# Products with V of four batches spread over four iterations in an attention and mixture-of-experts kernel

## The chip, the cores and the metric

The kernel runs on one core of a Trainium2 chip. The metric is the device time of one launch in microseconds (us). The core has a matrix engine (TensorE, PE in the rows; PEld are its weight loads), a vector engine (VectorE, DVE), a scalar engine (ScalarE, ACT), GpSimd (POOL) and a queue engine for transfers (SyncE, SP). Each engine runs its own instructions in program order, and they wait for each other by semaphores.

## What is computed

Attention with masks over 8 batches of 8 heads (576 positions, head size 64), then a top-1 mixture of 8 experts over the 4608 rows. Four heads see a local window of 32 positions, four see every 32nd position:

```python
scores = scale * np.matmul(q, k.transpose(0, 1, 3, 2))
mask_local = (rel >= 0) & (rel < stride)
mask_strided = (rel >= 0) & (pos[None, :] % stride == pos[:, None] % stride)
...
attn = np.exp(scores - max) / (sum + 1e-09)
attn_out = np.matmul(attn, v)
...
expert_idx = np.argmax(x @ w_gate, axis=1)        # x: attn_out, 4608 x 512
out[mask] = gate_w[mask, None] * (np.maximum(xe @ w1[e], 0.0) @ w2[e])
```

## The kernel before

**Attention** is cut into 40 tasks, five per batch (`tasks`, k = 0 to 4). Task k fills one score bank of 128 x 512: k = 0 and 1 are the two pairs of local heads, k = 2 is mixed, k = 3 and 4 are strided and their scores are issued together (`PAIR`). The loop runs one iteration per task as a software pipeline. In iteration i PE issues the transposes of the probabilities of task i - 3 (`stage_t`, `L501`), the scores of task i (`stage_s`, `L439` for the mask and `L450`, `L458`, `L464`), and the products with V of task i - 4: both pairs of local heads at k = 1 (`av_local`, `L526`), the first strided products at k = 3 and the second at k = 4 (`av_strided`, `L515`). So the products of batch b are issued while the scores of batch b + 1 are. PE's order is the order written in the code; the other engines are ordered by the scheduler.

**Softmax** of one bank: DVE takes the maximum (`nm`, `L377`) and subtracts it (`L380`, after which the score bank is free), ACT the exponential (`L381`), DVE the sum (`sm`, `L383`) and its reciprocal (`ri`, `L385`, `L386`), POOL the product (`L387`). Only then may PE transpose the probabilities. ACT copies each transposed bank (`pTl` for local heads, two copies of 64 x 512; `pT` for the others) and the products into `xT` (`L166`). There are two PSUM banks for each of the tags s (scores), t (transposes and first expert layer), v and y.

**Row work.** When all products of a batch are in `xT`, `row_steps` puts steps into `queue`: logits (`L576`), a copy `ls` by DVE (`L162`), a sum of transposed logits on PE (`L583`), rows transposed back and written to the buffer `xd` (`L568`, `L571`), and after every second batch the routing (`route`: counts with `oh`, then `am`, `bm` and `bb` on DVE, `L647` to `L659`, and the routing sum on PE, `L666`). `step()` runs one step, four times per iteration. A step that is only `single()` is a pause. For batches 0, 1, 2 the list goes to `late` and joins `queue` one iteration later, between the second and the third step of that iteration.

**Experts.** After batch 3 the first expert windows start inside the attention loop (`fillers`): gathers from `xd`, transposes (`L296`), weight chunks loaded by SP (`raw`), split by ACT and DVE into `whi` and `wlo` (`L231`, `L232`, two halves per chunk), and matmuls (`L309` to `L322`). Behind the attention loop the other windows follow.

Of the kernel before, what the change touches and what calls it, by code (L numbers as in the profile page):

```python
# [18 lines left out]
B, S, D = 8, 576, 64  # L19
# [9 lines left out]
GB = 2  # L29
# [23 lines left out]
TB = 5  # L53
EG = NG // 2
EARLY = (3, 1, 2)
X_ENG = "aa"
LS_ENG = "v"
BANKS = {"s": 2, "t": 2, "v": 2, "y": 2}
# [89 lines left out]
def moe_attn(ctx, tc, qk, vv, wg, wcat, blob0, blob, out):  # L148
# [8 lines left out]
    def bank(tag):  # L157
        return ps.tile([128, 512], F32, name=tag, bufs=BANKS[tag])

    def evac(which, out, in_):  # L160
        if which == "v":
            nc.vector.tensor_copy(out=out, in_=in_)  # L162
        elif which == "g":
            nc.gpsimd.tensor_copy(out=out, in_=in_)
        else:
            copied[0] = nc.scalar.copy(out=out, in_=in_)  # L166
# [178 lines left out]
    with ExitStack() as actx:  # L345
# [83 lines left out]
        def v_of(b, k, key, n=0):  # L429
            o = VV[k][0][key] + 128 * n  # L430
            return loaded[b, "v", k][:, o:o + 128]

        def side(k, h):

            return 1 - h if k == PAIR[1] else h
# [74 lines left out]
        def probs_of(b, pair, y, c, w):  # L510
            k, n = WHERE[pair]
            return pTs[b, k][64 * y:64 * y + 64, 128 * n + c:128 * n + c + w]

        def av_mm(av, c0, w, h, y, lhsT, rhs):
            nc.tensor.matmul(av[64 * h:64 * h + 64, c0:c0 + w], lhsT, rhs, start=True, stop=True, tile_position=(64 * y, 64 * h))  # L515

        def av_local(b, xT, off):
            for hp in range(2):
                av = bank("v")
                for m in range(2):  # L520
                    for i in range(4):
                        vt = v_of(b, hp, "l", 4 * m + i)
                        for h in range(2):
                            c = 128 * (2 * m + h) + QB * i
                            o = av[64 * h:64 * h + 64, 256 * m:256 * m + 256].rearrange("p (y r) -> p y r", y=2)
                            nc.tensor.matmul(o[:, :, QB * i:QB * i + QB], vt[:, 64 * h:64 * h + 64],  # L526
                                             pTl[hp][:, :, c:c + QB], start=True, stop=True, tile_position=(0, 64 * h))
                evac("a", xT[:, hp, off:off + 512], av)

        def av_strided(b, hp, xT, off):  # L530
            av = [bank("v"), bank("v")]
            for t in range(5):
                vst = v_of(b, WHERE["s", hp, t][0], ("s", hp, t))
                for y in range(2):
                    for h in range(2):
                        av_mm(av[y], RG * t, RG, h, y, vst[64 * y:64 * y + RG, 64 * h:64 * h + 64],
                              probs_of(b, ("s", hp, t), y, 64 * side(WHERE["s", hp, t][0], h), RG)[0:RG])
            c1 = 5 * RG
            if hp == 0:
                for i in range(2):  # L540
                    vt = v_of(b, 2, ("lx", i))
                    for y in range(2):
                        for h in range(2):
                            av_mm(av[y], c1 + QB * i, QB, h, y, vt[64 * y:64 * y + 64, 64 * h:64 * h + 64],
                                  probs_of(b, ("lx", 0, 4), y, 64 * h + 32 * i, 32))
            else:
                vst = v_of(b, 3, "sx")
                for y in range(2):
                    for h in range(2):
                        av_mm(av[y], c1, LASTG, h, y, vst[64 * y:64 * y + LASTG, 64 * h:64 * h + 64],  # L550
                              probs_of(b, ("sx", 0, 5), y, 64 * h, LASTG)[0:LASTG])
            xv = xT[:, 2 + hp, off:off + S].rearrange("p (a r) -> p r a", r=STR)
            for y in range(2):
                dst = xv[:, 0:30, :].rearrange("p (t y l) a -> p t y l a", y=2, l=3)[:, :, y, :, :]
                evac("a", dst, av[y][:, 0:c1].rearrange("p (t l a) -> p t l a", l=3, a=SR))
                if hp == 0:
                    x0 = off + 512 + QB * y
                    evac("a", xT[:, 0:2, x0:x0 + QB], av[y][:, c1:c1 + 2 * QB].rearrange("p (a q) -> p a q", q=QB))
                else:
                    xl = xT[:, 2 + y, off:off + S].rearrange("p (a r) -> p r a", r=STR)  # L560
                    evac("a", xl[:, 30:32, :], av[y][:, c1:c1 + LASTG].rearrange("p (r a) -> p r a", a=SR))

        def xrows(g, c, xT):
# [3 lines left out]
            for pr in range(4):  # L567
                nc.tensor.transpose(xb[:, pr * 128:(pr + 1) * 128], xT[:, pr, c * 128:(c + 1) * 128], ident)  # L568
            evac(X_ENG[c % 2], xr[:, 0:DM], xb)
            T = g * GT + c  # L570
# [272 lines left out]
        xTs = {}  # L843
        Ls = {}
        queue = []
        late = []

        def run(gen):
            for _ in gen:
# [2 lines left out]
        def one(fn, *a):  # L852
            fn(*a)
            yield
# [10 lines left out]
        def row_steps(g, bb, xT, L):  # L865
            lg = [logits(g, c3, xT, L) for c3 in range(bb, 1 if bb == 0 else GT // 3)]
            rows = [one(xrows, g, c, xT) for c in range(3 * bb, 3 if bb == 0 else GT)]
            last = g == NG - 1 and bb == GB - 1
            pause = [] if last or g * GB + bb < EG * GB - 1 else [single()]
            steps = list(pause)  # L870
            for r in range(3):
                steps += [part(x) for x in lg]
                if r == 0:
                    steps += [single()] if bb == 0 else pause
            if last:
                steps += rows + [route(g)]
            elif bb == GB - 1:
                steps.append(mix(route(g), rows))
                if g == EG - 1:
                    steps.append(one(lambda: fill.append(fillers())))  # L880
            else:
                steps += [x for r in rows for x in (r, single())]
            return steps
# [11 lines left out]
        def single():  # L895
            yield
# [32 lines left out]
        with tc.manual_schedule(engines={mybir.EngineType.PE}):  # L929
            for i in range(nt + LAG_AV):  # L930
                it = i - LAG_T
                if 0 <= it < nt:
                    stage_t(*tasks[it], pvs.pop(it))
                step()
                ia = i - LAG_AV
                if 0 <= ia < nt:
                    b, k = tasks[ia]
                    g, bb = divmod(b, GB)
                    if g not in xTs:
                        xTs[g] = xtp.tile([128, 4, GB * S], F32, name="xT")  # L940
                        Ls[g] = rt.tile([128, GT, E], F32, name="L", bufs=2)
                        dls[g] = rt.tile([128, GT, E], F32, name="dl", bufs=2)
                        gates[g] = rt.tile([128, GT], F32, name="gt", bufs=2)
                    step()
                exps.clear()
                if i < nt:
                    filling()
                    b, k = tasks[i]
                    if k == PAIR[0]:
                        pvs[i], pvs[i + 1] = stage_s(b, *PAIR)  # L950
                    elif k not in PAIR:
                        pvs[i], = stage_s(b, k)
                    load_qk(i + NBK)
                if 0 <= ia < nt:
                    b, k = tasks[ia]
                    if k == 0:
                        queue.extend(late)
                        late.clear()
                    elif k == 1:
                        av_local(b, xTs[g], bb * S)  # L960
                    elif k == 3:
                        av_strided(b, 0, xTs[g], bb * S)
                        for e in exps:
                            issue_after(e, copied[0])
                    elif k == 4:
                        av_strided(b, 1, xTs[g], bb * S)
                        for e in exps:
                            issue_after(e, copied[0])
                        (late if b < EG * GB - 1 else queue).extend(row_steps(g, bb, xTs[g], Ls[g]))
                        if b == B - 1:  # L970
                            filling()
                if 0 <= ia:
                    load_v(ia + NV - 1)
                step()
                filling()
                step()
# [5 lines left out]
        chain = queue.pop()  # L982
        for n in EARLY:
            with tc.high_priority():
# [326 lines left out]
```

## Time and profile before

| | |
|---|---|
| median of 3 runs | 626.51 us (624.65 to 626.82) |
| the profiled execution | 627.64 us, its span 625.9 us |
| PE busy in the span | 591.8 us (95%) |
| DVE, ACT, POOL busy | 374.8 (60%), 296.1 (47%), 160.4 us (26%) |
| mean granted clock of PE | 0.989 |

A row of a view gives a start or a stretch in us from the start of the span, a duration, an engine, a source line and the tiles written and read. Idle time stands with the engine and tile that ended it (`<-`). Rows that a prediction needs stand in a section of their own below.

### The profile page before, as it was taken

To read this page: it belongs to the slowest core of one execution; us is meant where nothing else is said; L and a number is where in the kernel's file an instruction comes from. 1 tells how busy PE (TensorE), PEld (TensorE's weight loads), DVE (VectorE), ACT (ScalarE), POOL (GpSimd) and SP (SyncE) were. 2 spreads that over 40 slices of the span, in tenths; PEclk is the share of its full clock that TensorE was granted. 3 is DMA by queue.
4 is the path that set the end of the run, shared out by engine and by line. 5 is a ranking of instruction groups with operands and counts; after the bars stand their busy time and mean duration, and the time that the engine had idled before them with its cause. 6 is when DMAs were issued, how large, how long until landed. Compare 5 with 4: busy or idle time off the path is not lost. (4 is left out here: it accounts for less than half of the span.)

```text
span 625.9 us, 14501 instructions
## 1 busy us (share of the span) xinstructions
PE 591.8 (95%) x5986; PEld 491.3 (78%) x5986; DVE 374.8 (60%) x744; ACT 296.1 (47%) x523; POOL 160.4 (26%) x195
## 2 busy tenths in 40 slices
PE   4998898789899999999999999999999999999996
PEld 2676767578778889887888898788998879887885
DVE  6778889886784689997325855233534335551332
ACT  1576667755566545475325744233433324442241
POOL 3333332441150303047302432022412004020021
PEclk9899899999899999999999999999999999999999
DMA  8788999995549566569934675375555538253201
GB/s 308 262 295 289 324 320 320 347 371 178 206 138 328 184 235 216 190 232 333 411 140 172 239 258 172 132 252 181 207 186 184 183 106 295 100 178 144 68 33 57
DMA packets 33540, 137.25 MB, mean 219 GB/s; under 512 B 4666, under 2 KB 5056, under 8 KB 24768
## 3 DMA queue, kind: packets, MB, share of 16 engines
q1 hardware_dynamic: 19840, 93.33, 43.4%
q10 hardware_dynamic: 7344, 22.71, 9.9%
q0 software_dynamic: 6288, 20.26, 8.8%
q8 instruction: 48, 0.79, 0.5%
q14 instruction: 20, 0.16, 0.1%
HBM read 117.11 MB, written 19.63 MB: 218 GB/s over the span
## 5 line engine op out<-in xcount | busy, mean ns | idle before, releaser
L232 DVE TENSOR_TENSOR wlo<-raw,whi 128x1024 fp32r<-128x1024 f32 x112 | 135.9, 1230 | 67.6 <-ACT whi L231 65.8
L231 ACT CAST whi<-raw 128x1024 fp32r<-128x1024 f32 x112 | 114.2, 1050 | 56.6 <-PE s L311 39.8
L320 PE MATMUL t<-xh,whi 128*128 128x256 f32 (+2 forms) x384 | 131.4, 343 | 2.1 <-DVE hl L326 1.5
L322 PE MATMUL t<-xh,wlo 128*128 128x256 f32 (+2 forms) x384 | 127.6, 332 | 0.0
L321 PE MATMUL t<-xl,whi 128*128 128x256 f32 (+2 forms) x384 | 127.5, 332 | 0.0
L326 DVE SCALAR_TENSOR_TENSOR hl<-t,hh 128x256 fp32r<-128x256 f32 (+2 forms) x96 | 52.1, 543 | 114.8 <-ACT hh L325 114.6
L325 ACT ACTIVATE hh<-t 128x256 fp32r<-128x256 f32 (+2 forms) x96 | 46.4, 483 | 133.3 <-PE t L322 129.6
L320 PEld LDWEIGHTS t<-xh,whi 128*128 128x128 f32 x384 | 72.2, 188 | 11.9 <-issue 3.2
L321 PEld LDWEIGHTS t<-xl,whi 128*128 128x128 f32 x384 | 72.3, 188 | 6.1 <-DVE xl L241 0.3
L310 PE MATMUL y<-wlo,hh 128*128 128x512 f32 x192 | 75.9, 396 | 0.9 <-DVE wlo L232 0.9
L309 PE MATMUL y<-whi,hh 128*128 128x512 f32 x192 | 76.6, 400 | 0.0
L322 PEld LDWEIGHTS t<-xh,wlo 128*128 128x128 f32 x384 | 72.3, 188 | 5.5 <-DVE wlo L232 0.2
L311 PE MATMUL y<-whi,hl 128*128 128x512 f32 x192 | 76.0, 397 | 0.3 <-DVE hl L326 0.3
L387 POOL TENSOR_TENSOR prob<-prob,ri 128x512 f32<-128x512 f32 x40 | 44.6, 1122 | 103.2 <-DVE ri L386 62.9
L277 POOL DMA_INDIRECT out_dram<-y,oids x27 | 29.7, 1099 | 102.9 <-DVE y L276 97.4
L249 POOL DMA_INDIRECT xg<-xd,ids x27 | 32.8, 1213 | 75.6 <-PE v L296 38.5
L311 PEld LDWEIGHTS y<-whi,hl 128*128 128x128 f32 x192 | 36.2, 189 | 8.9 <-DVE hl L326 1.5
L310 PEld LDWEIGHTS y<-wlo,hh 128*128 128x128 f32 x192 | 36.3, 190 | 6.5 <-DVE wlo L232 1.4
L309 PEld LDWEIGHTS y<-whi,hh 128*128 128x128 f32 x192 | 36.3, 190 | 5.7
L166 ACT COPY xT<-v 128x270 f32<-128x270 f32 (+1 forms) x80 | 29.2, 484 | 20.2 <-PE v L515 10.2
L310 PE MATMUL s<-wlo,hh 128*128 128x512 f32 x88 | 34.6, 393 | 0.0
L311 PE MATMUL s<-whi,hl 128*128 128x512 f32 x88 | 34.4, 391 | 0.0
(226 smaller groups left out, 905.2 us busy)
## 6 DMA issues: line engine op xcount, KB each, us to landing
raw<-in_wcat_dram SPq DMA_DIRECT2D x56, 1024.0 KB, 5.5
sraw<-in_wcat_dram ACTq DMA_DIRECT2D x12, 1024.0 KB, 5.0
xd<-xr ACTq DMA_DIRECT2D x36, 264.0 KB, 4.1
qkl<-in_qk_dram SPq DMA_DIRECT2D x32, 264.0 KB, 4.6
vl<-in_vv_dram SPq DMA_DIRECT2D x16, 512.0 KB, 5.8
vt<-in_vv_dram SPq DMA_DIRECT2D x16, 256.0 KB, 5.3
qk<-in_qk_dram SPq DMA_DIRECT2D x8, 484.0 KB, 6.5
qk<-in_qk_dram SPq DMA_DIRECT2D x8, 432.0 KB, 5.9
```

The costliest lines, as they stand in the source:

```text
L231: nc.scalar.copy(out=hi[:, sl], in_=raw[:, sl])
L232: i = nc.vector.tensor_tensor(out=lo[:, sl], in0=raw[:, sl], in1=hi[:, sl].bitcast(F32), op=ALU.subtract)
L249: lastp[0] = nc.gpsimd.indirect_dma_start(out=xg, out_offset=None, in_=xd[0:rows, :], in_offset=bass.IndirectOffsetOnAxis(ap=idc, axis=0))
L309: nc.tensor.matmul(yb[t], hh[:, ts], whi[:, w], start=(j == 0), stop=False)
L310: nc.tensor.matmul(yb[t], hh[:, ts], wlo[:, w], start=False, stop=False)
L311: nc.tensor.matmul(yb[t], hl[:, ts], whi[:, w], start=False, stop=(j == 7))
L320: nc.tensor.matmul(hb[:, 0:n], whi[:, w], xh[:, dc, :], start=(dc == 0), stop=False)
L321: nc.tensor.matmul(hb[:, 0:n], whi[:, w], xl[:, dc, :], start=False, stop=False)
L322: nc.tensor.matmul(hb[:, 0:n], wlo[:, w], xh[:, dc, :], start=False, stop=(dc == 3))
L325: nc.scalar.activation(out=hh[:, 0:n], in_=hb[:, 0:n], func=AF.Relu)
L326: nc.vector.scalar_tensor_tensor(out=hl[:, 0:n], in0=hb[:, 0:n], scalar=0.0, in1=hh[:, 0:n].bitcast(F32), op0=ALU.max, op1=ALU.subtract)
L387: product[0] = nc.gpsimd.tensor_tensor(out=pv, in0=pv, in1=ri.unsqueeze(2).broadcast_to([128, 8, 64]), op=ALU.mult)
```

## The change

For the batches named in `SPREAD` (0, 1, 2 and 4) the products with V are issued in other iterations. The first pair of local heads stays at k = 1, the second goes to k = 2. The first strided products stay at k = 3. The second go from k = 4 to k = 0 of the next batch, the iteration that issues no scores because they were issued together with those before. `row_steps` joins `queue` in that iteration too, and starts with four pauses, one iteration's worth of steps. `late` is gone; batches 3, 5, 6 and 7 are treated as before. At k = 4 of the four batches, no order between the exponentials and the last copy into `xT` is set any more.

```diff
+SPREAD = (0, 1, 2, 4)
...
-        def av_local(b, xT, off):
-            for hp in range(2):
+        def av_local(b, xT, off, *hps):
+            for hp in hps:
...
-            steps = list(pause)
+            steps = [single() for _ in range(4)] if g * GB + bb in SPREAD else list(pause)
...
                     if k == 0:
-                        queue.extend(late)
-                        late.clear()
+                        if b - 1 in SPREAD:
+                            pg, pb = divmod(b - 1, GB)
+                            av_strided(b - 1, 1, xTs[pg], pb * S)
+                            queue.extend(row_steps(pg, pb, xTs[pg], Ls[pg]))
                     elif k == 1:
-                        av_local(b, xTs[g], bb * S)
+                        av_local(b, xTs[g], bb * S, *((0,) if b in SPREAD else (0, 1)))
+                    elif k == 2:
+                        if b in SPREAD:
+                            av_local(b, xTs[g], bb * S, 1)
...
-                    elif k == 4:
+                    elif k == 4 and b not in SPREAD:
                         av_strided(b, 1, xTs[g], bb * S)
...
-                        (late if b < EG * GB - 1 else queue).extend(row_steps(g, bb, xTs[g], Ls[g]))
+                        queue.extend(row_steps(g, bb, xTs[g], Ls[g]))
```

PE behind the paired scores of batch 1, before: `v<-pT` are the second strided products of batch 0, `y<-xT,wg_sb` its logits, `y<-cst_70,ls` the sum of them, `v<-pTl` local products of batch 1, `y<-cst_70,xT` a row.

```order
L464 MATMUL s<-qk 54x54 x10
L515 MATMUL v<-pT,vt 64x54 x20
L515 MATMUL v<-pT,vt 64x36 x4
L501 MATMUL t<-cst_70,prob 128x128 x4
L576 MATMUL y<-xT,wg_sb 32x384 x4
L501 MATMUL t<-cst_70,prob 128x128 x4
L583 MATMUL y<-cst_70,ls 128x128 x3
L439 LDWEIGHTS identb
L439 MATMUL s<-mask_b,identb 128x512
L450 MATMUL s<-qkl_135 32x2x64 x16
L526 MATMUL v<-pTl_137,vl 64x2x32 x16
L526 MATMUL v<-pTl_138,vl 64x2x32 x16
```

The same place now (the lines have moved by one).

```order
L502 MATMUL t<-cst_70,prob 128x128 x4
L516 MATMUL v<-pT,vt 64x54 x20
L516 MATMUL v<-pT,vt 64x36 x4
L502 MATMUL t<-cst_70,prob 128x128 x4
L440 LDWEIGHTS identb
L440 MATMUL s<-mask_b,identb 128x512
L451 MATMUL s<-qkl_135 32x2x64 x16
L527 MATMUL v<-pTl_137,vl 64x2x32 x16
L577 MATMUL y<-xT,wg_sb 32x384 x4
L502 MATMUL t<-cst_70,prob 128x128 x4
L584 MATMUL y<-cst_70,ls 128x128 x3
```

A transpose now stands between the paired scores and the second strided products, the logits stand behind the first local products, and the second local products behind the next scores.

ACT at the same place, before: the four copies of the strided products into `xT`, then the two exponentials of the paired scores.

```order
L166 COPY pTl_137<-t 64x512 x2
L166 COPY xT<-v 128x5x3x18
L166 COPY xT<-v 128x2x18
L166 COPY xT<-v 128x5x3x18
L166 COPY xT<-v 128x2x18
L381 ACTIVATE prob<-prob 128x512
L166 COPY pTl_138<-t 64x512
L381 ACTIVATE prob<-prob 128x512
```

And now:

```order
L167 COPY pTl_137<-t 64x512 x2
L167 COPY pTl_138<-t 64x512 x2
L167 COPY xT<-v 128x5x3x18
L382 ACTIVATE prob<-prob 128x512
L167 COPY xT<-v 128x2x18
L382 ACTIVATE prob<-prob 128x512
L167 COPY xT<-v 128x5x3x18
L167 COPY xT<-v 128x2x18
```

All four copies of transposed local probabilities come ahead of the exponentials, and the copies into `xT` stand between and behind them.

DVE at the routing of batches 2 and 3 (`am`, `bm`, `bb`), where the scores of batch 5 are taken through softmax, before:

```order
L647 TENSOR_TENSOR am<-cst,pfall 128x1152
L380 TENSOR_TENSOR prob<-s,nm 128x512
L232 TENSOR_TENSOR wlo<-raw,whi 128x1024
L652 TENSOR_TENSOR bm<-cst,key 128x360
L657 TENSOR_TENSOR bb<-bm,cst 128x9x40
L659 TENSOR_SCALAR bb<-bm,cst 128x9x40
L380 TENSOR_TENSOR prob<-s,nm 128x512 x2
```

And now:

```order
L381 TENSOR_TENSOR prob<-s,nm 128x512
L233 TENSOR_TENSOR wlo<-raw,whi 128x1024
L648 TENSOR_TENSOR am<-cst,pfall 128x1152
L653 TENSOR_TENSOR bm<-cst,key 128x360
L387 RECIPROCAL ri<-ri 128x8
L378 TENSOR_REDUCE nm<-s 128x8 x2
L381 TENSOR_TENSOR prob<-s,nm 128x512 x2
L658 TENSOR_TENSOR bb<-bm,cst 128x9x40
L660 TENSOR_SCALAR bb<-bm,cst 128x9x40
```

The subtraction of the k = 2 scores moves ahead of `am`, and the maxima and subtractions of the paired scores move ahead of `bb`.

## Rows read from the trace of the kernel before

**Rows 1.** Stretches: us, PE busy (x), PEld, DVE, ACT, POOL, PEclk, DMA share, GB/s

```profile
20.00:60.00 40.00, 37.22 (x911) 27.88 (x912) 32.36 (x88) 27.38 (x60) 13.68 (x20) 0.98 0.86 284
60.00:100.00 40.00, 35.81 (x827) 27.10 (x827) 33.57 (x99) 27.53 (x60) 13.43 (x20) 0.96 0.94 321
100.00:130.00 30.00, 24.40 (x638) 19.09 (x637) 26.90 (x64) 21.88 (x46) 11.64 (x13) 1.00 0.98 340
...
97.00:116.00 19.00, 14.96 (x374) 11.12 (x373) 18.32 (x47) 14.10 (x29) 5.00 (x5) 1.00 0.96 325
```

**Rows 2.** Waits of PE, 20 to 165 us: releaser: us in total, times, longest

```profile
PE s L439 <- DVE prob L380: 2.7, 4, 1.6
PE t L501 <- POOL prob L387: 2.2, 3, 0.8
PE y L583 <- DVE ls L162: 1.3, 2, 0.8
PE v L296 <- ACT xT L166: 1.2, 1, 1.2
PE y L576 <- ACT xr L166: 1.2, 1, 1.2
PE v L583 <- DVE ls L162: 1.1, 1, 1.1
PE y L618 <- DVE ri L385: 0.9, 1, 0.9
...
PE v L576 <- ACT xT L166: 0.7, 1, 0.7
...
PE y L568 <- ACT xr L166: 0.5, 1, 0.5
```

**Rows 3.** Timeline of PE, logits: start, us, form, count, idle before

```profile
34.23 1.59 PE L576 MATMUL y<-xT,wg_sb 128*32 128x384 f32 x8
...
49.88 2.25 PE L576 MATMUL y<-xT,wg_sb 128*32 128x384 f32 x16
...
86.98 2.18 PE L576 MATMUL y<-xT,wg_sb 128*32 128x384 f32 x8
...
110.43 1.39 PE L576 MATMUL v<-xT,wg_sb 128*32 128x384 f32 x8 [0.70 <-ACT xT L166]
...
132.66 0.85 PE L576 MATMUL v<-xT,wg_sb 128*32 128x384 f32 x8
```

**Rows 4.** Timeline of PE at batch 0's local products

```profile
22.39 2.09 PE L526 MATMUL v<-pTl,vl 128*64 128x64 f32 x64
25.28 0.66 PE L501 MATMUL t<-cst,prob 128*128 128x128 f32 x4 [0.80 <-POOL prob L387]
```

**Rows 5.** Stretches of 2 us around 74 us, columns as in rows 1

```profile
72.00:74.00 2.00, 2.00 (x21) 0.74 (x25) 1.93 (x8) 1.96 (x4) 1.04 (x1) 0.62 1.03 404
74.00:76.00 2.00, 2.00 (x44) 1.56 (x38) 0.63 (x2) 0.09 (x1) 1.04 (x1) 0.53 1.05 393
```

**Rows 6.** Groups by line: shapes, count | busy us, mean ns | idle before

```profile
L387 POOL TENSOR_TENSOR prob<-prob,ri 128x512 f32<-128x512 f32 x40 | 44.6, 1122 | 103.2 <-DVE ri L386 62.9 <-DVE ri L385 16.4 <-ACT xT L166 8.9
...
L380 DVE TENSOR_TENSOR prob<-s,nm 128x512 f32<-128x512 f32 x40 | 26.6, 683 | 0.5
...
L377 DVE TENSOR_REDUCE nm<-s 128x8 f32<-128x512 f32 x40 | 26.5, 678 | 9.1 <-PE s L450 6.4 <-PE s L464 2.5
L381 ACT ACTIVATE prob<-prob 128x512 f32<-128x512 f32 x40 | 24.9, 631 | 19.9 <-DVE prob L380 19.9
...
L166 ACT COPY pTl<-t 64x512 f32<-64x512 f32 x32 | 18.5, 577 | 8.0 <-PE t L501 7.5 <-issue 0.3
```

**Rows 7.** Timeline of DVE at the routing of batches 2 and 3

```profile
103.07 1.22 DVE L232 TENSOR_TENSOR wlo<-raw,whi 128x1024 fp32r<-128x1024 f32 x1
...
106.58 1.13 DVE L657 TENSOR_TENSOR bb<-bm,cst 128x360 bf16<-128x360 f32 x1
107.63 0.57 DVE L659 TENSOR_SCALAR bb<-bm,cst 128x360 bf16<-128x360 f32 x1
```

More of the change, by code (lines that the diff above doesn't have):

```diff
@@ L845, in moe_attn @@
         queue = []
-        late = []
         def run(gen):
```

## Prediction, made before the change was run

> **What bounds the kernel now.** I read the stages first: busy time by stretch [rows 1]. Three phases show. From 20 to 130 us attention runs alone, then expert windows are threaded into it, then experts run by themselves. In attention TensorE (PE) is busy 37.2 of 40, 35.8 of 40 and 24.4 of 30 us, so it stands still for 2.8, 4.2 and 5.6 us; VectorE (DVE) is at 32 to 34 of 40 us, and in 97 to 116 us it is full, 18.32 of 19. DMA shares are 0.86 to 0.98, but no wait of PE in 20 to 165 us names a load, so the transfers run ahead of use. The matrix work itself is not changed, so only PE's waits can be won.
>
> Second, who PE waits for in 20 to 165 us [rows 2]. The nine longest entries come to 11.8 us: 2.7 for the score bank (PE `L439` waits until DVE's subtraction `L380` has read the bank), 2.2 for POOL's product that makes the probabilities (`L501`), 1.3 and 1.1 for the copy `ls` (`L583`), and row and `xT` copies.
>
> Third, waits that the busy time hides. A logits group (`L576`, 8 records) takes 0.85 us when its data is there; directly behind the second strided products it takes 1.59, 2.18 and 1.39 us, and a double one 2.25 instead of 1.70 [rows 3]. That is 0.74 + 1.33 + 0.54 + 0.55 = 3.2 us in which PE waits for ScalarE's (ACT) copies into `xT`.
>
> The Trainium skill, page Perfetto Trace Analysis, section Identifying the Most-Contended Engine, says the matmul busy share is no measure of PE's headroom and the weight-load share should be read. Rows 1 give 27.9, 27.1 and 19.1 us of loads in the same three stretches, 36 us of room by that reading against 12.6 by the busy time; the logits groups agree that busy time hides waits, 3.2 us of them.
>
> **The change part by part.** Nothing is computed anew: every matmul, copy and transfer keeps its size. What moves on PE is one local product (pair 1, half of the 2.09 us of [rows 4], so 1.0) by one iteration, the second strided products by one iteration, and the row work (logits, `ls` sums, transposed rows) by about one. The added instructions are none; the four pauses issue nothing. I follow PE in its new order and let each wait end when the producing engine, in its own new order, is done.
>
> Removed. Of the 11.8 us, 0.8 of `L501` stays (the wait in [rows 4], below), and the waits `L296` (1.2) and `v L583` (1.1) come at the first expert window, where DVE's copies stand just as tightly after the change; I count them as staying. So 8.7 us go. The 3.2 hidden in logits go too, since the logits now come one iteration later, when ACT has long copied. And the slow clock goes: in 72 to 74 and 74 to 76 us the granted clock was 0.62 and 0.53 [rows 5], right behind the wait for `L501` at 69 us and the 1.2 us of `L576`, both among those removed; 2 x 0.38 + 2 x 0.47 = 1.7 us lost. Removed in all: 8.7 + 3.2 + 1.7 = 13.6 us.
>
> Added: what takes the place of the removed cover. The paired scores end a chain that the next iterations depend on: DVE takes two maxima and two subtractions (0.68 each), ACT two exponentials (0.63 each), DVE two sums and the reciprocals, POOL two products (1.12 each) [rows 6]; only then may PE transpose. Today the strided products, a transpose, the logits, another transpose, the `ls` sum, the scores, both local halves and a row cover that chain; after the change the `ls` sum, one local half and the row stand behind the transpose.
> - Batch 0, at its first transposed pair: PE now waits 0.80 us for the product [rows 4]. The chain is not earlier, but 1.0 us of local products has left the cover: +1.0.
> - Batch 0, at its strided iteration: ACT evacuates four half tiles `pTl` (4 x 0.58 = 2.3 us, [rows 6]) before the first exponential, where it evacuated four `xT` pieces before; DVE now takes the sum of the k=2 scores ahead of the two paired maxima. PE then waits 0.5 (third transpose), 0.4 (score bank) and, at the next transpose, which PE reaches 6.1 us after the paired scores while the product ends 7.0 us after them (four `pTl` 2.3, a strided piece and a wait 0.6, two exponentials 1.4, a sum 0.7, a maximum and reciprocals 0.9, the product 1.1), 0.9. Together +1.8.
> - Batch 1, the same places with two logits groups (1.70) in the cover instead of one: 0.2 + 0.35 + 0.25, and 0.8 because the second `ls` copy stands behind the next subtraction: +1.6.
> - Batch 2, where batch 1's routing runs: DVE holds the one-hot product and both halves of the table ahead of the paired subtractions, as now. PE arrives some 2 us earlier at a DVE that is no earlier: 1.05 at the score bank and 1.05 at the transpose, +2.1.
> - Batch 3, not spread itself: the `ls` copy stands behind both exponentials: +0.75.
> - Batch 4, the costliest place. Routing of batches 2 and 3 puts a one-hot product, two halves of a weight split (1.22 each, one row shown) and the table (`bb`, 1.13 and 0.57) on DVE [rows 7], which is full there [rows 1]. In the new DVE order both halves of the weight split and the two paired maxima and subtractions (2 x 0.68 + 2 x 0.68 = 2.7) stand before `bb`; before, one half and the paired four came behind it. So `bb` is done about 1.6 us later than today's 108.2, near 109.8 (one split half and the four come ahead of it, 3.9 us; DVE starts on the stretch 2.3 us earlier, as PE's earlier waits are gone), while PE, some 5 us ahead by then, is at the transpose before the routing sum at 104.3. It waits 2.45 there (reciprocal behind `bm`) and 2.55 at the routing sum: +5.0.
> Behind that the first expert window starts with the same two waits as now.
>
> Added in all: 1.0 + 1.8 + 1.6 + 2.1 + 0.75 + 5.0 = 12.25 us. Net: 12.25 - 13.6 = -1.3 us against the profiled execution's 627.64, so 626.3; that execution lies 1.1 above the median of the runs shown, so **625.2** on their scale.
>
> Bounds of what the trace does not show. The added waits are sums of a few rows each and could be half as long or a quarter longer: -6.1 or +3.1 us on the net. A new stretch of half clock behind the 5.0 us of batch 4 would cost 1.7, as at 72 us; I take 0, since in 97 to 116 us, which hold today's waits of 1.6, 0.7 and 0.8 us, the clock was at full speed ([rows 1, 2]), and keep 1.7 in the range. SP's queue: the value load that waits for the second strided products now waits one iteration longer, and the next batch's loads stand behind it; they have an iteration or more to spare, so nothing, and at worst a part of a us where the first weight chunk lands.
>
> **The rivals.**
> - A, DVE gives way earlier. If DVE finishes the routing table about when it does now in order (its removed waits pass to it as well), the 5.0 of batch 4 becomes 1.5 and the two transposes of batches 0 and 1 lose half: net -1.3 - 3.5 - 1.2 = -6, **620.5**. For: in 20 to 100 us DVE has 6 to 8 us free per 40. Against: 18.32 of 19 in 97 to 116.
> - B, ACT decides, and the kernel is slower. If ACT really holds the paired exponentials behind the four `pTl` evacuations and a strided piece, each spread batch's product ends 1.3 us later than I counted, and all four transposes wait for it: +5.2 - 1.3 = +3.9, **630.4**. It decides where an exponential starts more than 2 us behind its DVE subtraction. For: the order on ACT. Against: ACT is busy 27 of 40 us.
> - C, waits only change their names: the sum is zero within 1 us, **626.5**. This lies in the forecast's own range.
> - D, busy time on PE is soft, and nothing comes back: -13.6, **612.9**. For: the hidden 3.2. Against: in [rows 4] a transpose keeps its 0.66 us behind a wait, so its time is its own. The page Perfetto Trace Analysis of the Trainium skill, in the section named above, would have it so.
>
> **How the numbers follow.** The forecast with C: 0.53. A: 0.28. B: 0.16. D: 0.03. A difference under 0.5% (3.1 us) is about what a measurement of this kernel can't tell from none; the forecast and C lie within it, A and D are faster, B slower. So faster 0.31, same 0.53, slower 0.16. The range takes most of A and all of B: 620.0 to 630.5.
>
> **What would show it.** In the profile after: the logits groups at 0.85 us each and no ACT wait at `L576`; PE's wait for DVE's subtraction near 107 us gone; in its place waits of `L501` for POOL growing from 2.2 to some 6 us and a wait at the routing sum of batches 2 and 3 for DVE of 2 us or more; the clock at 72 to 76 us at 1.0; the first expert matmul 1 to 3 us earlier than now. Wrong if `L501` does not wait more (A), if the exponentials of the paired scores start late and the waits for POOL pass 10 us (B), or if PE waits for a load.

## The result: slower by 1.15%

The changed kernel takes 633.67 us (median of 4 runs, 631.12 to 634.53) against 626.33 us beside it: ratio 1.0115, interval 1.0081 to 1.015, some 7.2 us. The forecast of 625.2, no change, is wrong, and so is the top of its range, 630.5. Run again on another chip the same kernel gave 1.0094 (1.0064 to 1.0124). All ratios below are to runs of the kernel before on the same chip.

The page of the profiled execution (633.66 us), its first lines: the engines are as busy as before, PE even 3 us less, in a span 6 us longer.

```profile
span 631.9 us, 14500 instructions
...
PE 589.0 (93%) x5986; PEld 490.2 (78%) x5986; DVE 374.5 (59%) x744; ACT 296.5 (47%) x523; POOL 156.3 (25%) x195
```

The stretches of [rows 1] after the change:

```profile
20.00:60.00 40.00, 34.09 (x892) 25.94 (x881) 30.86 (x85) 24.70 (x55) 14.11 (x18) 1.00 0.82 280
60.00:100.00 40.00, 35.43 (x835) 27.19 (x833) 33.14 (x95) 28.06 (x60) 12.25 (x23) 0.96 0.94 315
100.00:130.00 30.00, 22.41 (x580) 17.84 (x579) 25.08 (x65) 20.22 (x42) 11.39 (x13) 0.94 0.92 314
97.00:116.00 19.00, 16.26 (x416) 13.43 (x416) 18.21 (x54) 14.03 (x29) 5.94 (x8) 1.00 0.97 344
```

PE's waits from 20 to 165 us after the change, to lay beside [rows 2]: the wait for DVE's subtraction (the score bank) is gone, the one for POOL's product has grown from 2.2 to 3.5, and on top stands one that the prediction does not have, 3.6 us in one piece for a copy `ls`.

```profile
PE v L584 <- DVE ls L163: 3.6, 1, 3.6
PE t L502 <- POOL prob L388: 3.5, 3, 1.7
PE v L569 <- ACT xT L167: 2.6, 3, 1.1
PE y L577 <- ACT xr L167: 2.1, 1, 2.1
...
PE y L667 <- DVE bb L660: 1.4, 1, 1.4
```

**Where the time went.** Busy time and waits do not add up by stretch here, since the same work stands in other stretches. So I worked out a lost time at each mark: the start of a mark in the trace, less the time of all PE work that stands ahead of it in program order, each group at its duration from start to next start where nothing holds it (scores 1.32 and 1.28 us with their mask, a local pair 1.04, strided 0.97 and 0.83, logits 0.80, twelve first-layer matmuls 1.42, six second-layer ones 1.40). What two kernels differ by is then waits and slow clock alone. Up to the first mark all five kernels do the same work in the same order, so the 1.9 us between them in the first row show how far one execution differs from another. The loss in each stretch, in us (the last two columns are experiments below):

| up to | before | after | after, second profile | later fillers only (`before_gap7`) | after with both causes removed (`after_both`) |
|---|---|---|---|---|---|
| first scores of batch 1 | 14.4 | 12.5 | 13.7 | 13.6 | 13.8 |
| paired scores of batch 5 | 15.1 | 15.3 | 13.6 | 14.4 | 14.9 |
| k = 2 scores of batch 6 | 3.2 | 6.9 | 8.2 | 3.2 | 4.0 |
| paired scores of batch 7 | 8.1 | 6.5 | 7.4 | 8.1 | 7.4 |
| last routing sum | 4.0 | 8.6 | 8.8 | 9.4 | 4.6 |
| end, against before | 0 | +1.0 | 0.0 | +0.5 | 0.0 |

Up to the paired scores of batch 5 (which start at 107 us before and at 104 after) nothing is lost. Two places lose: 3.7 and 5.0 us by the k = 2 scores of batch 6, and 4.6 to 4.8 us between the last paired scores and the last routing sum.

**The first place.** DVE after the change (start, duration, line, operation, output and input, idle before and who ended it):

```profile
117.10 0.64 DVE L378 TENSOR_REDUCE nm<-s 128x8 f32<-128x512 f32 x1
119.33 1.23 DVE L233 TENSOR_TENSOR wlo<-raw,whi 128x1024 fp32r<-128x1024 f32 x1 [1.59 <-ACT whi L232]
120.47 0.69 DVE L381 TENSOR_TENSOR prob<-s,nm 128x512 f32<-128x512 f32 x1
121.07 0.55 DVE L163 COPY ls<-v 128x384 f32<-128x384 f32 x1
```

ACT, the cast that the split `wlo` waits for:

```profile
118.25 1.99 ACT L232 CAST whi<-raw 128x1024 fp32r<-128x1024 f32 x2 [0.85 <-DMA raw<-in_wcat_dram]
```

SP, the issue of that weight chunk:

```profile
109.66 0.33 SPq L222 DMA_DIRECT2D raw<-in_wcat_dram  x1
```

and PE, which wants `ls` of batch 4:

```profile
121.77 0.52 PE L584 MATMUL v<-cst,ls 128*128 128x128 f32 x3 [3.62 <-DVE ls L163]
```

It is a chain of four queues. The second early weight chunk is issued at 109.66 and is there at about 118.2. ACT casts it; DVE, whose order now has the split `wlo` ahead of the subtraction and of `ls`, stands still for it; PE stands 3.62 us for a copy of 0.55 us whose input it had finished at 117.6. Before the change batch 4's row work came earlier and its `ls` stood well ahead of that split. DVE then:

```profile
112.74 0.55 DVE L162 COPY ls<-v 128x384 f32<-128x384 f32 x1
...
120.63 1.26 DVE L232 TENSOR_TENSOR wlo<-raw,whi 128x1024 fp32r<-128x1024 f32 x1 [1.26 <-ACT whi L231]
```

The Trainium skill, page PSUM — Partial Sum Buffer, section Engine vs sequencer instructions, calls the queues of ScalarE, VectorE and GpSimd strict FIFO; the rows agree, a copy that was ready at 117.6 starts at 121.07. Behind the wait PE runs at half its clock (stretches of 2 us, columns as in [rows 1]):

```profile
122.00:124.00 2.00, 2.00 (x46) 1.51 (x48) 1.63 (x4) 0.00 (x0) 1.59 (x1) 0.65 0.61 199
124.00:126.00 2.00, 1.72 (x62) 1.58 (x58) 1.70 (x5) 0.23 (x1) 0.72 (x1) 0.50 0.64 165
```

**The second place.** The fillers are pulled at fixed points of an iteration, two each, and start when the routing steps of batches 2 and 3 have left `queue`. The pauses make that one iteration later. In program order 56 groups of first-layer matmuls stand ahead of the last strided product before, 48 after. The first expert matmul starts at 129.69 us before, and after:

```profile
136.56 0.39 PE L321 MATMUL t<-xh,whi 128*128 128x256 f32 x1
```

The prediction had this matmul 1 to 3 us earlier than before. So 5.6 us of expert work (24 matmuls of 0.118, 12 of 0.233) leave the attention loop; it ends 4.6 us earlier (last strided product done at 197.6 instead of 202.2), and the work is done later. That alone would be even but for about 1 us. But the next expert window now meets the last row work and routing in another position. PE's waits from 197 to 232 us before:

```profile
PE y L310 <- DVE wlo L232: 0.9, 1, 0.9
```

and after:

```profile
PE y L312 <- DVE hl L327: 1.8, 1, 1.8
PE y L310 <- ACT hh L326: 0.9, 1, 0.9
PE v L569 <- ACT xr L167: 0.7, 1, 0.7
```

Two halves of the window's hidden layer (`hh` by ACT, `hl` by DVE) now fall behind ACT's row copies, where the issue of two transfers holds ACT's queue for 3.01 us, and behind DVE's routing (`hl` starts at 224.29, at the end of `am` and `key`). ACT there:

```profile
215.62 3.01 ACTq L572 DMA_DIRECT2D xd<-xr  x2
218.73 0.59 ACT L167 COPY xr<-v 128x512 f32<-128x512 f32 x1 [2.71 <-issue]
...
221.35 0.66 ACT L326 ACTIVATE hh<-t 128x256 fp32r<-128x256 f32 x2 [0.46 <-DVE cnt L625]
```

And here too half clock follows the waits:

```profile
224.00:226.00 2.00, 1.24 (x4) 1.04 (x5) 2.00 (x7) 0.00 (x0) 0.00 (x0) 0.75 0.51 143
226.00:228.00 2.00, 2.00 (x10) 1.29 (x9) 1.55 (x2) 0.00 (x0) 0.00 (x0) 0.50 0.00 0
```

### The profile page after: what moved, and what is told of

Same layout as the page of the kernel before. It is cut to its first block, busy times and chain, and to the rows that moved or that the text cites. A ratio compares the mean times of both kernels' runs of the same rounds, so it can differ in the third digit from the quotient of the medians.

```text
span 631.9 us, 14500 instructions
## 1 busy us (share of the span) xinstructions
PE 589.0 (93%) x5986; PEld 490.2 (78%) x5986; DVE 374.5 (59%) x744; ACT 296.5 (47%) x523; POOL 156.3 (25%) x195
## 5 line engine op out<-in xcount | busy, mean ns | idle before, releaser
L388 POOL TENSOR_TENSOR prob<-prob,ri 128x512 f32<-128x512 f32 x40 | 41.7, 1048 | 91.9 <-DVE ri L387 44.9
L384 DVE TENSOR_REDUCE sm<-prob 128x8 f32<-128x512 f32 x40 | 26.7, 681 | 14.1 <-ACT prob L382 14.1
```

Of the source, the lines that this page charges most:

```text
L388: product[0] = nc.gpsimd.tensor_tensor(out=pv, in0=pv, in1=ri.unsqueeze(2).broadcast_to([128, 8, 64]), op=ALU.mult)
```

## The experiments

The theories in the order in which they came: S, it is the later start of the fillers; A, the spread products themselves cost. After the first runs: W, the weight split ahead of `ls`; R, the later row work; P, the moved products. At last F, the position of the expert window against the last routing, and H, many small losses. Each expectation states its theory in full.

### Moving the start of the fillers alone

The kernel before with two more empty steps (`before_gap7`), the changed kernel with two fewer (`after_gap3`):

```diff
             cur = make(EXP[0])
-            for _ in range(5):
+            for _ in range(7):
                 yield
```

> The kernel before with seven empty steps instead of five at the start of the fillers: attention is untouched, the expert matmuls begin one iteration later (48 groups instead of 56 ahead of the last strided product). Theory S: 626.3 + 5 = 631.3 us, between 630 and 633. Theory A: 626.3 us, within 1.

Measured 1.0046 (1.0016 to 1.0076), 2.9 us: a loss without any product moved, but less than the 5 us of S. The table shows it at the last routing sum: 9.4 us where before has 4.0.

> The changed kernel with the five empty steps at the start of the fillers cut to three, so that the expert matmuls stand in the same iterations of the attention loop as before the change (56 groups of four first-layer products ahead of the last strided product, as in the kernel before, instead of 48). Theory S (the change lets the fillers begin one iteration later; the 5.6 us of expert work that leave the attention loop are done behind it in a stretch that has waits of 3.4 us instead of 0.9 and a stretch of half clock): 633.7 - 5 = 628.5 us, between 627 and 630, and the stretch 200 to 240 us without the waits for hh and hl. Theory A (the spread products cost their waits inside the attention loop, and where expert work stands is neutral): 633.7 us, within 1.5.

Measured 1.0181 (1.0144 to 1.0218): worse than the change, against both theories. The expert matmuls stand in their old iterations, but the profile loses 9 us between the paired scores of batch 7 and the end that before does not lose. S as it stood has fallen: it is not the iteration alone. Why this mixture is the worse is not settled.

### Leaving batches out

```diff
-SPREAD = (0, 1, 2, 4)
+SPREAD = (0, 1, 4)
```

> The changed kernel with batch 2 taken out of SPREAD; the fillers then begin in the same iteration as before the change (56 groups). Theory S: 627 us, within 1.5. Theory A: three quarters of the loss stay, 631.8 us, within 1.5.

> The changed kernel with batch 4 taken out of SPREAD; the fillers begin one iteration later, as in the changed kernel (48 groups). Theory S: 632.5 us, within 1.5, some 5.5 above the run without batch 2. Theory A: three quarters of the loss, 631.8 us, the same as the run without batch 2 within 1.5; less, towards 628, if batch 4's two waits are the costly ones, as the prediction had it.

Measured 1.0195 (1.0156 to 1.0233) and 1.0109 (1.006 to 1.0158). S had the first of them at next to no loss; it is the slower of the two. So there is more than the fillers.

For the next runs the list of a batch that is not spread joins as before the change (`late` put back):

```diff
+        late = []
...
                     if k == 0:
+                        queue.extend(late)
+                        late.clear()
                         if b - 1 in SPREAD:
...
-                        queue.extend(row_steps(g, bb, xTs[g], Ls[g]))
+                        (late if b < EG * GB - 1 else queue).extend(row_steps(g, bb, xTs[g], Ls[g]))
```

> Only batch 4 is spread; the lists of batches 0 to 2 join the queue as before the change. The fillers begin as before, and ls of batch 4 stands ahead of the second chunk's wlo on DVE. Theory W: 1.000, within 0.003, since neither of the two costs is there. Theory A: 1.003 to 1.005 (of four spread batches one, the one that the prediction gave the largest waits).

> Only batches 0 and 1 are spread, the list of batch 2 as before the change. Fillers as before. Theory W: 1.000, within 0.003. Theory A: 1.005.

> Batches 0, 1 and 4 are spread, the list of batch 2 as before the change (the earlier run without batch 2 let that list join an iteration earlier). Fillers as before, but on DVE one wlo of the second chunk stands ahead of ls of batch 4, as in the changed kernel. Theory W: 1.006 to 1.008, a wait of PE of 3 us or more for ls near 118 us. Theory A: 1.008, but without such a wait.

Measured 1.0087 (1.0059 to 1.0115), 1.0116 (1.0088 to 1.0145) and 1.0172 (1.0136 to 1.0207). W had the first two at 1.000, and A had all three at half of what was measured or less. The last is in fact a repeat of `spread014`: with batch 1's list still in the queue, PE, DVE and ACT get the same order either way, and the ratios agree. So parts of the spread cost without either of the two places above. With batch 4 alone PE's largest new wait is at the logits of batch 5:

```profile
135.20 2.03 PE L577 MATMUL v<-xT,wg_sb 128*32 128x384 f32 x8 [2.63 <-ACT xT L167]
```

ACT makes the copies into `xT` behind a weight cast that waits for its chunk, which SP issued at 125.36 us (111.57 before). It is what happened at the first place, with ACT's queue instead of DVE's:

```profile
133.51 1.04 ACT L232 CAST whi<-raw 128x1024 fp32r<-128x1024 f32 x1 [4.21 <-DMA raw<-in_wcat_dram]
134.46 1.23 ACT L167 COPY xT<-v 128x270 f32<-128x270 f32 x4
```

With batches 0 and 1 alone a row waits for ACT (PE); ACT's copy `xr` stands behind an exponential that itself waited 2.52 us for DVE's subtraction:

```profile
75.09 1.11 PE L569 MATMUL y<-cst,xT 128*128 128x128 f32 x4 [3.50 <-ACT xr L167]
```

All four together cost less than these parts added (0.87 and 1.16 are 2.03%, the change has 1.15%), so the prices of parts do not add up; which order of batch 2 makes the difference was not tried by itself.

### `ls` ahead of the weight split

```diff
+            lscopy.append(nc.vector.tensor_copy(out=out, in_=in_))
...
+            if turn2[0] == 1:
+                issue_after(i, lscopy[6])
+        turn2[0] += 1
```

Here `i` is the split `wlo` of the chunk with the number `turn2`, and `lscopy[6]` is `ls` of batch 4. PE's order stays word for word.

> The changed kernel with one order set on DVE: both subtractions wlo of the second early weight chunk stand behind the copy ls of batch 4, as they do before the change; PE's order is untouched. Theory W (in the changed kernel ls stands behind wlo, which waits for ACT's cast, which waits for the transfer of that weight chunk; PE waits 3.6 us for ls at 118 us and then has 3 us at half clock): the wait goes, ratio to the kernel before 1.004 to 1.006 instead of 1.0115. Theory A (the spread products cost their waits in many places): 1.0115, within 0.003.

Measured 1.0082 (1.0051 to 1.0113). Compared with 1.0115 and 1.0094 that is 0.1 to 0.3% less: the sign of W but not its size, and the intervals overlap, so this run alone shows no gain. In its profile the wait for `ls` is 0.18 us.

### Rows alone, products alone

```diff
-            steps = list(pause)
+            steps = [single() for _ in range({0: 4, 1: 4, 2: 4, 4: 8}[g * GB + bb])] if g * GB + bb in (0, 1, 2, 4) else list(pause)
```

> The kernel before with all products where they were; only the row lists of batches 0, 1, 2 and 4 begin as late as in the changed kernel (pauses added), so that logits, sums and rows, and with them the fillers, stand in the same iterations of PE as after the change. Theory R (it is the later row work and the later fillers that cost): 1.008 to 1.012, as the whole change. Theory P (the moved products cost): 1.003 to 1.006, the price of the later fillers alone, as in the run with seven empty steps (1.0046).

Measured 1.023 (1.0184 to 1.0276), twice the loss of the change. With the row work as late as the change has it and the products where they were, the kernel is worse than with both moved. Its profile loses most of that between the paired scores of batch 7 and the last strided product, where PE waits 1.65 us for `xl` on DVE, behind the routing of batches 4 and 5, and then runs at half clock (0.50 from 178 to 182 us).

The changed kernel with `range(2)` in place of `range(4)` in its pauses:

> The changed kernel with two pauses instead of four ahead of the row work: the products are spread as in the change, the rows come half an iteration earlier, the fillers begin in the same iteration as before the change, and ls of batch 4 stands ahead of the second chunk's wlo on DVE. Theory R: 1.000 to 1.003. Theory P: 1.007 to 1.012.

Measured 1.0207 (1.017 to 1.0243). R fell with this: rows half an iteration earlier and fillers as before, and yet slower than the change. P has the sign, at half of what was measured. Neither of the two places is in its trace (its waits for `ls` are 0.5 us at most, and 56 groups stand ahead of the last strided product). Worked out as in the table, it loses 8.5 us more than the kernel before between the first scores of batch 1 and the paired scores of batch 5: logits that now stand closer behind the copies into `xT` wait 1.95 and 2.10 us for them, a transpose 2.38 us for POOL, and the waits for the score bank (1.28 and 1.10 us) are back. So the attention loop too can lose by a small move; that it does not in the change hangs on the four pauses.

```diff
-        def av_local(b, xT, off):
-            for hp in range(2):
+        def av_local(b, xT, off, *hps):
+            for hp in hps:
...
-                        av_local(b, xTs[g], bb * S)
+                        av_local(b, xTs[g], bb * S, *((0,) if b in SPREAD else (0, 1)))
+                    elif k == 2:
+                        if b in SPREAD:
+                            av_local(b, xTs[g], bb * S, 1)
```

> Only the second pair of local products of batches 0, 1, 2 and 4 moves from k = 1 to k = 2; strided products, row lists and fillers are as before. Theory R: 1.000, within 0.003. Theory P: 1.003 to 1.006, from waits of PE for POOL's product behind the shorter cover.

Measured 1.0035 (1.0005 to 1.0064), at the lower end of P and just outside R, with an interval that reaches into both.

> The changed kernel once more, beside the three on the same chip. Both theories: 1.0115, within 0.003; its stretches of half clock (88, 122 and 224 us in its first profile) stand in the same places only if a certain wait starts each of them.

Measured 1.0094 (1.0064 to 1.0124). In its profile the stretches of low clock stand at 14 to 18, 88 to 94, 110 to 118, 124 to 132 and 226 to 230 us: those at 88, 124 and 226 are, within 2 us, in both profiles, behind the 2.12 us wait of the logits of batch 3 (both), the wait for `ls` (3.62 and 2.09) and the tail's waits. The others come and go.

### The tail's order put back

Two more pulls behind the last scores, so that from the last strided product on PE's order is that of the kernel before:

```diff
                     load_qk(i + NBK)
+                elif i < nt + 2:
+                    filling()
                 if 0 <= ia < nt:
```

> The changed kernel with two more pulls of expert work in the first two iterations behind the last scores, so that from the last strided product on PE's order is exactly that of the kernel before (56 groups done instead of 48); all before is as changed. Theory F (the fillers that begin one iteration later shift the expert work against the last routing, and that stretch, last paired scores to last routing sum, loses 8.6 us instead of 4.0): ratio 1.003 to 1.006 instead of 1.0115 and 1.0094, and that stretch near 4. Theory H (the loss is spread over waits and half-clock stretches everywhere; the tail only shows them): 1.010, within 0.003.

> The kernel before with seven empty steps at the start of the fillers and the same two pulls more behind the last scores. Theory F: 1.000 to 1.002 instead of 1.0046. Theory H: 1.0046, within 0.003.

> The changed kernel with both: ls of batch 4 ahead of the second chunk's wlo on DVE, and the two pulls more behind the last scores. Theories W and F together: 1.000 to 1.003. Theory H: 1.008, as with ls first alone (1.0082).

Measured 1.0077 (1.0052 to 1.0101), 0.9996 (0.9973 to 1.0019) and 1.0001 (0.9978 to 1.0024). The first lies above F's range and inside H's, though its waits for `hh` and `hl` are gone. The second fits F: what the later fillers cost by themselves goes with the tail's order (the intervals of 1.0046 and 0.9996 just touch). The third is the answer to the case: with `ls` ahead of the split and the tail's order put back, nothing is left of the loss, although every product and every row stands in the attention loop as the change puts it. H, which had 1.008 for it, is out. The stretch from 197 to 232 us of the four kernels shows it (PE busy stands behind the length); before:

```profile
197.00:232.00 35.00, 34.02 (x339) 28.48 (x337) 23.73 (x67) 19.86 (x38) 6.04 (x10) 1.00 0.64 224
```

after:

```profile
197.00:232.00 35.00, 31.64 (x258) 26.13 (x251) 21.13 (x58) 16.93 (x31) 5.05 (x10) 0.95 0.53 183
```

later fillers alone (`before_gap7`):

```profile
197.00:232.00 35.00, 32.31 (x214) 26.26 (x213) 21.99 (x60) 16.35 (x29) 5.05 (x10) 0.90 0.51 179
```

and `after_both`:

```profile
197.00:232.00 35.00, 33.73 (x331) 28.33 (x332) 23.15 (x67) 18.93 (x37) 6.02 (x10) 1.00 0.59 199
```

The waits for `hh` and `hl` are gone from `after_both`, the clock is full, and `ls` is in time, on DVE ahead of the split:

```profile
119.06 0.55 DVE L163 COPY ls<-v 128x384 f32<-128x384 f32 x1
119.52 0.68 DVE L386 TENSOR_TENSOR prob<-s,nm 128x512 f32<-128x512 f32 x1
...
120.49 1.23 DVE L235 TENSOR_TENSOR wlo<-raw,whi 128x1024 fp32r<-128x1024 f32 x1
```

> The kernel before with later row lists alone (1.023) and the two pulls more behind the last scores. In its profile the stretch from the last paired scores to the last routing sum lost 16.8 us instead of 4.0. Theory F: 1.004 to 1.009. Theory H: 1.02.

Measured 1.0196 (1.0157 to 1.0235) against 1.023 without the pulls. The two pulls do not help the later rows alone: worked out as in the table, they still lose some 10 us more than before between the last paired scores and the last routing sum, and the 1.64 us wait for `xl` ahead of it stays. F is not their cause, and it was not followed further.

> The kernel before with the two pulls more behind the last scores: 64 groups of expert work ahead of the last strided product instead of 56. If it is a deficit of expert work in the attention loop that costs (theory F1), more of it gains or does nothing: 0.995 to 1.000. If it is the position of the expert window against the last routing (theory F2), any shift from 56 can cost: 1.002 to 1.010.

Measured 1.0036 (1.0017 to 1.0055). The kernel before is shifted the other way here, with more expert work done ahead of the tail, and it costs as well. So it is not a lack of expert work in the loop. But its profile does not show F's place either: up to the last routing sum it loses no more than the kernel before. It loses some 4 us far behind it, where PE waits 1.6 us in three pieces for a gather and then has a low clock:

```profile
290.22 0.33 PE L296 MATMUL v<-cst,xg 128*128 128x128 f32 x1 [0.93 <-DMA xg<-xd,ids]
...
292.00:296.00 4.00, 3.76 (x16) 2.96 (x15) 3.33 (x4) 3.44 (x6) 3.39 (x3) 0.57 1.02 396
```

## Why the prediction was wrong

**The sum for the attention loop came out near, its two halves did not.** Forecast up to the first expert window: 13.6 us removed, 12.25 added, -1.3. `after_both`, the whole change without its two accidents, stands at 1.0001, which leaves room for -1.4 to +1.5 us. Split at the paired scores of batch 5, the forecast is 11.6 removed against 7.25 added ahead of them, -4.4, and 2.0 removed (the 0.7, 0.75 and 0.54 us at 110 to 113 us) against 5.0 added behind them, +3.0. Measured by the table's second row: 15.3, 13.6 and 14.9 us lost with the products spread against 15.1 and 14.4 in two kernels without, so nothing to 1 us won ahead of that mark; and behind it, up to the k = 2 scores of batch 6, 4.0 in `after_both` against 3.2, +0.8. Two misses of some 4 and 2 us took each other away, so that the sum came near is in part luck. Rival C, waits only change their names, is what happened there.

- Removed, right: the wait for the score bank is gone; the logits behind spread batches take 0.85, 1.50 (double) and 0.85 us where [rows 3] had 1.59 and 2.25 for the first two; no stretch from 72 to 76 us has a low clock. Batch 3, not spread, gets a 2.12 us wait ahead of its logits in place of the hidden one; the 1.45 us that they take here are half clock (0.62 and 0.53 from 88 to 92 us), in the second profile they take 0.85 behind the same wait.

```profile
36.35 0.85 PE L577 MATMUL y<-xT,wg_sb 128*32 128x384 f32 x8
...
54.58 1.50 PE L577 MATMUL y<-xT,wg_sb 128*32 128x384 f32 x16
...
78.23 0.85 PE L577 MATMUL y<-xT,wg_sb 128*32 128x384 f32 x8
...
88.37 1.45 PE L577 MATMUL y<-xT,wg_sb 128*32 128x384 f32 x8 [2.12 <-ACT xr L167]
```

- Added, near in size: batch 0's first transposed pair 1.70 (forecast 0.80 + 1.0), the later one 1.08 (0.9). Batch 1 has 1.37 and 0.20 in this profile (forecast 1.6), but the 1.37 name no engine and are not in the second profile. Batch 2's 2.1 for DVE did not show; 1.01 and 1.45 us for ACT's copies (at 65.47 and 73.50) stand there instead.

```profile
23.34 0.66 PE L502 MATMUL t<-cst,prob 128*128 128x128 f32 x4 [1.70 <-POOL prob L388]
...
38.29 0.66 PE L502 MATMUL t<-cst,prob 128*128 128x128 f32 x4 [1.08 <-POOL prob L388]
```

- Added, wrong: batch 3's 0.75 for `ls` were 2.12 at the logits, for ACT's `xr`. Batch 4's 5.0 us were 0.69 at the transpose and 1.42 at the routing sum, 2.1 in all. That is close to the 1.5 of rival A, but not for A's reason: DVE was done with `bb` at 110.90, later than the 109.8 of the forecast. PE was later still: it stood at the transpose at 108.2, not at 104.3, which fits the gain ahead of this place that had not come.

```profile
110.32 0.58 DVE L660 TENSOR_SCALAR bb<-bm,cst 128x360 bf16<-128x360 f32 x1
...
108.89 0.66 PE L502 MATMUL t<-cst,prob 128*128 128x128 f32 x4 [0.69 <-POOL prob L388]
110.96 0.50 PE L667 MATMUL y<-bb,am 128*128 128x80 bf16 x9 [1.42 <-DVE bb L660]
```

One reading of the rows was off: the nine entries of [rows 2] that make 11.8 us are not the nine longest, since a wait of 0.6 us of the row work for ACT's `xT` and 0.8 us that name no engine are longer than the last of them.

**The step that failed** is the sentence "Behind that the first expert window starts with the same two waits as now", and with it the one on SP's queue that let the first weight chunk cost "at worst a part of a us". I followed the moved row work to its last matmul in the attention loop and stopped there. Two things hang on it beyond. First, the start of the fillers stands behind the same list, so the pauses move all expert work by an iteration, and what that meets behind 200 us, at the last routing, was never looked at; the number of expert groups ahead of the last strided product, 56 before and 48 after, was there to be counted in the order of PE. It is worth 2.9 us by itself (1.0046) and 4.6 to 4.8 in the two profiles of the change. Second, `ls` of batch 4 moved behind a weight split on DVE whose input is a transfer that landed 8.6 us after its issue. I asked whether the load is later, which it is not; I should have asked what on DVE is queued behind its split. It shows as 3.62 and 2.09 us. Taken out one at a time the two give back 0.1 to 0.3% and 0.2 to 0.4%, taken out together 0.9 to 1.1%; by the intervals the sizes of the single ones are loose, and whether they add up or need each other stays open; the joint one is clear.

Rival B (ACT holds the paired exponentials) named the right sign and the wrong place: waits for POOL came to 3.5 and 4.6 us in the two profiles, not the 10 that it asked for. Rival D, that busy time on PE is soft and the removed 13.6 us all come back, is out: `after_both` has the changed order in the attention loop and stands at 1.0001. The Trainium skill, page Perfetto Trace Analysis, section Identifying the Most-Contended Engine, names the weight-load share as one of two measures of PE's room. By the prediction's estimate from that share the room is 36 us; no run here gained any of it, and the loads take 78% of the span before and after.

**What stays open.** The two accidents account for this change, not for its relatives. Batch 4 alone, batches 0 and 1 alone and the change with two pauses (1.0087, 1.0116 and 1.0207) have neither and lose about as much or more; the waits named above are in their traces. Why later rows alone (1.023) cost twice the change was not followed to its end. With two fewer empty steps (1.0181) PE waits 2.01 us for `hh` at 298 us, far behind the last routing; in `local_only` it waits 1.91 us for `hh` at 292 us. No run put these orders back, so a cause is not shown for them.

## What to carry to other kernels

In a software pipeline whose side work starts when a list runs empty, a change that moves the list moves everything that starts behind it: count, in the order of the bounding engine, how much of the side work stands ahead of the last mark, and look at what it meets there. On an in-order engine ask of every step that moves which waiting instruction now stands ahead of it; the two here that waited for a transfer (a split on DVE, a cast on ACT) held PE for 3.62 and 2.63 us, and the transfer did not come earlier because the rest did. And when such a kernel gets slower, put the accidental orders back, one by one and then together, before blaming the idea: here each alone gave 0.4% at most, both gave all of it.

## What the runs showed of the chip

PE's clock drops to half (a granted clock of 0.50) behind waits, and not each time: behind the 3.62 us wait of the first profile it did, behind the 1.70 us one at 23 us it did not. Between two profiles of the same changed kernel the time lost by it, busy time times the missing share summed over stretches of 2 us, was 4.7 and 10.1 us, while both runs took 633.7 and 634.7 us. Waits and slow clock can trade against each other: with the clock at half from 110 to 118 us, PE came later to `ls` and waited 2.09 us instead of 3.62. PE's listed waits are no measure of a loss by themselves: from 20 to 165 us they add up to 13.4 us before, to 20.9 after and to 18.6 in `after_both`, which is no slower than before. The lost time at a mark puts `after_both` beside the kernel before, the list of waits does not.
